# A softmax add on GpSimd, and two preparations moved behind later attention units

## The chip, the core and the metric

The kernel runs on one core of a Trainium2 chip. The core has TensorE (PE, matrix products into PSUM; its weight loads are shown as PEld), VectorE (DVE), ScalarE (ACT), GpSimd (POOL) and SyncE (SP, which here issues nearly all DMAs). Each engine works through its own instructions in order; between engines semaphores hold an instruction until its operands are there. The metric is the time on the device in microseconds. Before the change it was 2141.11 us, the median of three runs from 2140.84 to 2141.45.

## The reference

Attention with a sink and a window, then a mixture of experts in which every expert sees every token and a Sinkhorn iteration makes the weights:

```python
# q, k, v: (4, 8, 768, 64): batches, heads, positions, head size
scores = scale * q @ k.T
keep = (column < 4) | (0 <= row - column < 128)     # sink, or window
a = exp(where(keep, scores, -1e9) - max)
a = a / (sum(a) + 1e-9)
x = (a @ v) laid out as 3072 tokens x 512
P = exp(x @ w_gate - max)
8 times: P /= rowsum + 1e-9; P /= columnsum + 1e-9; P *= 3072 / 8
out = sum over 8 experts e of P[:, e] * (relu(x @ w1[e]) @ w2[e])   # w1: 512 x 1024, w2: 1024 x 512
```

## The kernel before

**Numbers.** Matrix products run on values in the fp32r format. Where full precision is wanted, a value is held as two halves, high and low: `split` (line 348) makes the high half with a copy on ScalarE and the low half as source minus high half on VectorE. A product is then three products (high-high, high-low, low-high).

**Attention units.** The attention works in 48 units: 4 batches, 6 blocks of 128 rows, and two halves of four heads (`units`, line 389). For a unit, `transpose_qk` transposes keys and queries of two pairs of heads in PE (L426) and splits them into the buffer KQ (high half L430 on ScalarE, low half L431 on VectorE). `scores` does two heads at a time (`pr` is 0 or 1): six products each pair (L461) of a row block with 260 columns (4 of the sink, 256 of two blocks), then per head a custom VectorE instruction that adds the mask, scales and finds the maximum (L464), then per head an exponential on ScalarE that also sums the row (L467), then 1e-9 is added to the two sums (L468), the reciprocal is taken (L469), and GpSimd multiplies the rows (L471). `transpose_p` transposes the scaled rows in PE (L482) and splits them (L350 is the line in `split`; the buffer is PT). `transpose_sinks` does the same for the sink columns (L496, L497 on GpSimd, L499 on PE, L501 on ScalarE). `values` multiplies with V (L520), which `split_v` splits on GpSimd (L440, L441), and copies the outcome to xr (L532), half on ScalarE and half on VectorE. `store_x` sends it to memory and, for the first third of the tokens, splits it into the blocks B (L540, L541).

**Order of the steps.** The loop from line 712 runs n from -2 to 50. A step n holds, in this order: loads for unit n+2; the scores of unit n+1; the first values of unit n-1; a piece of the fill; a piece of the gate; the transposes of keys and queries of unit n+2; the transposed probabilities of unit n; the second values of n-1; the sinks of n; a second piece of the fill. PE's instructions are issued in exactly this written order (`manual_schedule`). On the other engines a planner sets the order: it plays the program through with its own costs and gives an engine that is free the instruction earliest in the program of those that are ready. `tc.issue_after(ins)` holds what is traced inside it behind `ins` on the engine of `ins`, and on that engine only. It is an order of issue, with no wait for the end of `ins`.

**The fill.** From n = 5 on (`START`) every step gives PE two pieces of the first expert's products (`plain`): products with W1 (L599), a rectified value split into h (L604 on ScalarE, L605 on VectorE), products with W2 (L615). An expert has four units of 256 columns; the fill takes units 0 and 1 first, then 2 and 3. `load_plain` loads a unit's raw W1 and W2 and splits them in four pieces, two of W1 and two of W2 (the buffers are W and W2f). For units 0 and 1 the pieces are held: W1's behind the splits of attention units 1 and 2, W2's behind those of units 3 and 4, on both engines, since both instructions of a split are named:

```python
for ins in us[1 + 2 * (j // 2) + u]["split"]:
    held_back.enter_context(tc.issue_after(ins))
split(d, r)
```

In the program they stand in step 5, where the fill makes its first piece. For units 2 and 3 nothing holds them.

**The gate.** For the first third of the tokens the routing products (L561) use weights split by `split_gate` (line 308): four 128x128 fills with zero (L310), the high half (L311), the low half (L312) and a small matrix `sel` (L313), all on VectorE. It stands at the start of step 2, held behind unit 1's split on VectorE. For later tokens the raw weights are used.

**After the attention** (from about 300 us) come the rest of the first expert and the others, in products of 512 columns (L784, L1028, L1343) with an order of steps that is written out for every engine. None of it is touched.

Of the kernel before, what the change touches and what calls it, by code (L numbers as in the profile page):

```python
# [12 lines left out]
ALU = mybir.AluOpType  # L13
# [216 lines left out]
def tile_sink_attention_moe(ctx: ExitStack, tc: tile.TileContext, q, k, v, wg, w1, w2, out):  # L230

    nc = tc.nc
    B, H, S, D = q.shape
    N, DM = out.shape
    E, _, FF = w1.shape
# [18 lines left out]
    def f32(ap):  # L254
        return ap.bitcast(F32)
# [52 lines left out]
    def split_gate():  # L308
        for kc in range(KC):
            nc.vector.tensor_copy(wgr[:, kc, :], zero)  # L310
        nc.vector.tensor_copy(wgr[:, :, 0:E], wg_raw)  # L311
        nc.vector.tensor_sub(wgr[:, :, E:2 * E], wg_raw, f32(wgr[:, :, 0:E]))  # L312
        nc.vector.tensor_add(sel, ident[0:2 * E, 0:E], ident[0:2 * E, E:2 * E])  # L313
# [27 lines left out]
    def load_raw(rawp, e, u):  # L341
        r1 = rawp.tile([P, KC, UF], F32, name="r1")
        nc.sync.dma_start(r1, w1[e].rearrange("(k p) f -> p k f", p=P)[:, :, u * UF:(u + 1) * UF])
        r2 = rawp.tile([P, 2, DM], F32, name="r2")
        nc.sync.dma_start(r2, w2[e, u * UF:(u + 1) * UF, :].rearrange("(c p) d -> p c d", p=P))
        return r1, r2

    def split(dst, src):

        return nc.scalar.copy(dst[:, 0], src).ins, nc.vector.tensor_sub(dst[:, 1], src, f32(dst[:, 0])).ins  # L350
# [39 lines left out]
    us = {}  # L390
# [4 lines left out]
    def load_sinks(b):  # L395
        vs = seq[b] = att.tile([SK, D], F32, name="vs")
        for r0 in range(0, SK, NK):
            (nc.sync if b else nc.scalar).dma_start(vs[r0:r0 + NK, :], v[b, :, 0:SINK, :])
# [10 lines left out]
    def load_block(b, i):  # L409
        raws[b, i] = r = [att.tile([P, H, D], F32, name=nm) for nm in ("kr", "qr", "vr")]  # L410
        cuts = (0, HH, H) if (b, i) == (0, 0) else (0, H)
        for ts in (((r[0], k), (r[1], q)), ((r[2], v),)):
            for h0, h1 in zip(cuts, cuts[1:]):
                for t, src in ts:
                    nc.sync.dma_start(t[:, h0:h1, :], src[b, h0:h1, i * P:(i + 1) * P, :].rearrange("h p d -> p h d"))
# [28 lines left out]
    def scores(n, pr):  # L444

        b, i, hh = units[n]
        u = us[n]
        K, Q = KQ[hh][:, :, :, 0:CW], KQ[hh][:, :, :, CW:][:, :, :, turn_of(b, i)]
        if pr == 0:
            u["sc"] = att.tile([P, HH, CW], F32, name="sc", bufs=3)  # L450
            u["st"] = att.tile([P, 3, HH], F32, name="st", bufs=3)
        sc = u["sc"]
        nmx, sm, rs = (u["st"][:, j, :] for j in range(3))
        hs = range(2 * pr, 2 * pr + 2)
        p2 = slice(2 * pr, 2 * pr + 2)
        ps = {h: ps_st.tile([P, CW], F32, name="st") for h in hs}

        for j, (a, c) in enumerate(((0, 0), (0, 1), (1, 0))):
            for h in hs:
                r0 = (h % 2) * D  # L460
                nc.tensor.matmul(ps[h], lhsT=Q[r0:r0 + D, a, pr, :], rhs=K[r0:r0 + D, c, pr, :],  # L461
                                 start=(j == 0), stop=(j == 2))
        for h in hs:
            nc.vector.tensor_tensor_reduce(out=sc[:, h, :], in0=ps[h], in1=masks[place(b, i).start, min(i, 2)], op0=ALU.add, op1=ALU.min,  # L464
                                           scale=-scale, scalar=3.0e38, accum_out=nmx[:, h:h + 1])
        for h in hs:
            nc.scalar.activation(sc[:, h, :], sc[:, h, :], AF.Exp, bias=nmx[:, h:h + 1], scale=-1.0, accum_out=sm[:, h:h + 1])  # L467
        nc.vector.tensor_scalar(rs[:, p2], sm[:, p2], 1e-9, None, op0=ALU.add)  # L468
        nc.vector.reciprocal(rs[:, p2], rs[:, p2])  # L469
        for h in hs:  # L470
            u["scaled"] = nc.gpsimd.tensor_scalar(sc[:, h, :], sc[:, h, :], rs[:, h:h + 1], 1.0, op0=ALU.mult, op1=ALU.mult).ins  # L471
# [102 lines left out]
    def gate_step():  # L574
        if gates and next(gates[0], 0) == 0:
            gates.pop(0)
            gate_step()

    def load_plain(e, u):

        r1, r2 = load_raw(rawp, e, u)
        W1 = wa.tile([P, 2, KC, UF], F32R, name="W1")
        W2 = w2pr.tile([P, 2, 2, DM], F32R, name="W2f")
        for j, (d, r) in enumerate(((W1[:, :, 0:KH], r1[:, 0:KH]), (W1[:, :, KH:], r1[:, KH:]), (W2[:, :, 0], r2[:, 0]), (W2[:, :, 1], r2[:, 1]))):
            with ExitStack() as held_back:
                if u < 2:

                    for ins in us[1 + 2 * (j // 2) + u]["split"]:
                        held_back.enter_context(tc.issue_after(ins))
                split(d, r)  # L590
        return W1, W2
# [62 lines left out]
    def run_fill(k_):  # L654
        for _ in range(k_):
            next(fill, None)
# [5 lines left out]
    def load1(n):  # L662
        e, u = units0[n]
        R1[n] = rawp.tile([P, KC, UF], F32, name="r1")
        nc.sync.dma_start(R1[n], w1[e].rearrange("(k p) f -> p k f", p=P)[:, :, u * UF:(u + 1) * UF])
# [10 lines left out]
    def sums1(n):  # L676

        A11, A12, A21, A22 = blocks(R1[n])
        if n not in ST:
            ST[n] = new_sums()  # L680
        S = ST[n]
        nc.gpsimd.tensor_add(S[:, 3], A21, A22)
        nc.gpsimd.tensor_sub(S[:, 0], S[:, 3], A11)
        nc.gpsimd.tensor_sub(S[:, 2], A11, A21)
        nc.gpsimd.tensor_sub(S[:, 1], A12, S[:, 0])

    def pieces1(n):

        if n not in ST:
            ST[n] = new_sums()  # L690
        W = W1F[n] = (w1p if n % 2 else w1r).tile([P, 2, 7, KH, P], F32R, name="W1f")
        return [(W[:, :, 0:2].rearrange("p w a k f -> p w (a k) f"), R1[n][:, :, 0:P]), (W[:, :, 2], blocks(R1[n])[3]),
                (W[:, :, 3:5], ST[n][:, 0:2]), (W[:, :, 5:7], ST[n][:, 2:4])]
# [3 lines left out]
    def first_w1(n):  # L697

        if n == L - 8:
            load1(0)  # L700
        elif n == L - 6:
            sums1(0)
            first_pieces.extend(pieces1(0))
        if n >= L - 6 and first_pieces:
            split(*first_pieces.pop(0))
# [5 lines left out]
    with tc.manual_schedule(engines={PE}):  # L711
        for n in range(-2, L + 3):
            on = lambda j: 0 <= j < L
            if on(n + 2):
                b, i, hh = units[n + 2]
                if hh == 0:
                    with (tc.high_priority() if n == -2 else nullcontext()):
                        load_block(b, i)
                    if i == 0:
                        load_sinks(b)  # L720
            if n == -2:
                nc.sync.dma_start(wg_raw, wg.rearrange("(k p) e -> p k e", p=P))
            if n == 2:
                with tc.issue_after(us[1]["split"][1]):
                    split_gate()
            gates += later
            later.clear()
            if on(n + 1):
                scores(n + 1, 0)
                scores(n + 1, 1)  # L730
            if on(n - 1):
                values(n - 1, 0)
            if n >= START:
                run_fill(1)
            gate_step()
            for j in (0, 1) if n == -2 else (n + 2,) if n >= 0 else ():
                if on(j):
                    transpose_qk(j)
            if on(n):
                transpose_p(n, 0)  # L740
                with (tc.issue_after(us[n - 1]["scaled"]) if n > 1 else nullcontext()):
                    split_v(n)
            gate_step()
            if on(n):
                transpose_p(n, 1)
            if on(n - 1):
                values(n - 1, 1)
            gate_step()
            if on(n) and units[n][1]:
                transpose_sinks(n)  # L750
            if on(n) and units[n][1:] == (0, 1):
                with tc.issue_after(us[n]["scaled"]):
                    split_sinks(units[n][0])
            if n >= START:
                run_fill(1)
            first_w1(n)
        while gates:
            gate_step()
# [760 lines left out]
```

## Time and profile before

| | us |
|---|---|
| median of three runs | 2141.11 (2140.84 to 2141.45) |
| the profiled execution | 2141.32 |
| its span, first to last instruction | 2139.5 |
| TensorE busy | 2120.6 (99%) |
| VectorE busy | 1538.2 (72%) |
| ScalarE busy | 883.0 (41%) |
| GpSimd busy | 752.4 (35%) |

Times in the profile are microseconds from the start of the span. A row of the order of time has the start, the duration, the engine, the line, the operation, output<-inputs, shapes and how many were merged; in brackets is the idle time of the engine just before it and who ended it. A row of a group has the count, then busy time in us and the mean of one in ns, then the engine's idle time before them with its releasers. A row of waits has the total in us, how often, and the longest.

### The profile page before, as it was taken

What the parts mean: (1) busy time and instruction counts of PE and PEld (TensorE: products, weight loads), DVE (VectorE), ACT (ScalarE), POOL (GpSimd) and SP (SyncE); (2) the same over time, 40 slices, a digit from 0 to 9 for tenths busy, and PEclk for the clock granted to TensorE, in tenths of its full rate; (3) what the DMA queues carried; (4) which work ended last, traced back from release to release, by engine and by line L of the source; (5) the groups of instructions that cost most, each with busy time, mean ns of one, the idle gap of its engine ahead of it and who ended that gap; (6) DMA issues with size and microseconds to landing.
All of it is one profiled execution on the core that took longest, in us unless ns stands there. A gap on an engine that the chain in (4) does not pass through costs nothing.

```text
span 2139.5 us, 31828 instructions
## 1 busy us (share of the span) xinstructions
PE 2120.6 (99%) x10501; PEld 1770.4 (83%) x10501; DVE 1538.2 (72%) x2821; ACT 883.0 (41%) x1867; POOL 752.4 (35%) x950
## 2 busy tenths in 40 slices
PE   8999999999999999999999999999999999999998
PEld 7898897888888888888888888888888888888887
DVE  9878878877777776766666666666656666676666
ACT  7777744444444444442333223332333223332222
POOL 7766643233232331232223222232423232233223
PEclk9999999999999999999999999999999999999999
DMA  7434326999998987686666666667866666666662
GB/s 184 96 81 103 85 80 223 320 300 315 295 315 286 313 287 251 219 278 209 201 191 204 206 193 205 202 200 260 300 205 194 200 206 193 201 207 189 205 197 85
DMA packets 397643, 453.83 MB, mean 212 GB/s; under 512 B 99680, under 2 KB 265760, under 8 KB 396576
## 3 DMA queue, kind: packets, MB, share of 16 engines
q1 hardware_dynamic: 397080, 451.57, 67.8%
q8 instruction: 86, 1.41, 0.3%
q14 instruction: 85, 0.70, 0.1%
q10 hardware_dynamic: 392, 0.16, 0.0%
HBM read 314.17 MB, written 137.46 MB: 211 GB/s over the span
## 4 chain that ended last, share of the span: by engine, by line
PE 93%; DVE 3%; ACT 2%; POOL 1%; issue 0%; DMA 0%; SPq 0%; DVEq 0%; ACTq 0%; POOLq 0%
PE c L784 41%; PE o L1343 20%; PE held L1343 8%; PE o L1028 7%; PE held L1028 7%; PE O L520 3%; PE st L461 2%; ACT sc L467 1%; PE o L615 1%; PE st L482 1%; PE g L599 1%; PE st L426 1%; DVE sc L464 0%; POOL sc L471 0%; DVE PT L350 0%
## 5 line engine op out<-in xcount | busy, mean ns | idle before, releaser
L810 ACT CAST hf<-w 128x512 fp32r<-128x512 f32 x448 | 265.5, 622 | 561.8 <-POOL w L1310 298.9
L1343 PE MATMUL o<-hf,W2q 128*128 128x512 f32 x1920 | 472.0, 389 | 0.0
L1343 PEld LDWEIGHTS o<-hf,W2q 128*128 128x128 f32 x1920 | 360.0, 188 | 75.5 <-DVE acc L1357 0.9
L784 PE MATMUL c<-T,W1q 128*128 128x512 f32 x1530 | 388.9, 389 | 0.2 <-DVE w L1291 0.2
L811 DVE TENSOR_TENSOR hf<-w,hf 128x512 fp32r<-128x512 f32 x448 | 329.3, 763 | 76.2 <-ACT hf L810 68.5
L784 PEld LDWEIGHTS c<-T,W1q 128*128 128x128 f32 x1530 | 286.8, 188 | 60.7 <-DVE w L1291 0.9
L1357 DVE TENSOR_TENSOR acc<-o,acc 128x512 f32<-128x512 f32 x298 | 204.7, 688 | 171.1 <-PE o L1343 171.1
L784 PE MATMUL c<-B,W1q 128*128 128x512 f32 x1134 | 278.3, 389 | 0.0
L1310 POOL TENSOR_TENSOR w<-w 128x512 f32<-128x512 f32 x64 | 82.7, 1293 | 491.6 <-DVE w L1292 491.6
L784 PEld LDWEIGHTS c<-B,W1q 128*128 128x128 f32 x1134 | 212.5, 188 | 44.0
L1291 DVE TENSOR_TENSOR w<-c,M 128x512 f32<-128x512 f32 x192 | 132.3, 689 | 138.0 <-PE c L784 132.6
L1287 ACT COPY M<-c 128x512 f32<-128x512 f32 x192 | 112.7, 587 | 249.4 <-PE c L784 249.3
L1343 PE MATMUL held<-hf,W2q 128*128 128x512 f32 x768 | 194.8, 389 | 0.0
L784 PE MATMUL c<-T,W1f 128*128 128x512 f32 x672 | 171.2, 390 | 0.1
L1028 PE MATMUL held<-W2f,h 128*128 128x512 f32 x672 | 171.1, 390 | 0.0
L1028 PE MATMUL o<-W2f,h 128*128 128x512 f32 x672 | 170.6, 389 | 0.1
L1343 PEld LDWEIGHTS held<-hf,W2q 128*128 128x128 f32 x768 | 144.0, 188 | 29.8
L1325 POOL TENSOR_TENSOR w<-w 128x512 f32<-128x512 f32 x64 | 106.3, 1661 | 176.0 <-DVE hf L811 176.0
L1028 PEld LDWEIGHTS o<-W2f,h 128*128 128x128 f32 x672 | 126.0, 188 | 27.0 <-DVE acc L1035 0.9
L784 PEld LDWEIGHTS c<-T,W1f 128*128 128x128 f32 x672 | 125.7, 188 | 27.0 <-issue 0.5
L1028 PEld LDWEIGHTS held<-W2f,h 128*128 128x128 f32 x672 | 125.8, 188 | 26.4 <-DVE W2f L811 0.5
L837 POOL TENSOR_TENSOR r<-r 128x256 f32<-128x256 f32 x27 | 20.1, 746 | 359.2 <-ACT M L991 223.1
(216 smaller groups left out, 3104.5 us busy)
## 6 DMA issues: line engine op xcount, KB each, us to landing
W2q<-w2s SPq DMA_DIRECT2D x448, 256.0 KB, 3.2
W1q<-w1s SPq DMA_DIRECT2D x444, 256.0 KB, 2.9
w1s<-W1f SPq DMA_DIRECT2D x56, 896.0 KB, 7.8
w2s<-WT SPq DMA_DIRECT2D x136, 256.0 KB, 3.5
r<-in_moe_w_dram SPq DMA_DIRECT2D x64, 512.0 KB, 3.9
w2s<-W2f SPq DMA_DIRECT2D x56, 256.0 KB, 4.8
PB<-psd SPq DMA_DIRECT2D x16, 512.0 KB, 4.1
w2s<-W2f SPq DMA_DIRECT2D x56, 128.0 KB, 6.5
```

Of the source, the lines that this page charges most:

```text
L461: nc.tensor.matmul(ps[h], lhsT=Q[r0:r0 + D, a, pr, :], rhs=K[r0:r0 + D, c, pr, :], start=(j == 0), stop=(j == 2))
L520: nc.tensor.matmul(u["O"][:, pr], lhsT=x_, rhs=y_, start=(j == 0), stop=(j == len(ops) - 1))
L784: nc.tensor.matmul(ps, lhsT=w1(a, k), rhs=x[:, b, k, :], start=(start and j == 0), stop=(stop and j == len(TERMS) - 1), skip_group_check=n ...
L810: nc.scalar.copy(dst[:, 0], src)
L811: at(1, lambda: nc.vector.tensor_sub(dst[:, 1], src, f32(dst[:, 0])))
L1028: nc.tensor.matmul(o, lhsT=h[c, th][:, a, off:off + P], rhs=W2F[n][:, w, c, :], start=(begin and c == 0 and j == 0), stop=(end and c == 1 ...
L1287: nc.scalar.copy(t, T["c2"])
L1291: nc.vector.tensor_add(w, T["c1"], T[m])
L1310: nc.gpsimd.tensor_sub(S3, T["A11"], T["A21"])
L1325: at(k, lambda: nc.gpsimd.tensor_sub(T["A11"], w, T["A11"]))
L1343: nc.tensor.matmul(o, lhsT=W2Q[part, n, m][:, a, k * P:(k + 1) * P], rhs=F[part, n, H_OF[m]][:, w, :], start=(j == 0 and (begin or not hol ...
L1357: nc.vector.tensor_add(sums[m, k], o, sums[m, k])
```

## The change

Two things are changed, all within the attention stage. First, the add of 1e-9 to the two sums is issued on GpSimd; the instruction has a second operation, a multiplication by 1.0. The reciprocal stays on VectorE. Second, preparations move. The four W2 pieces of units 0 and 1 of the first expert are no longer traced with their W1 pieces but put in a list, `second_pieces`; at the end of step 5 the two of unit 0 are split, at the end of step 6 the two of unit 1, held behind `us[n]["split"][1]`, the VectorE instruction of attention unit n's last split. The W1 pieces stay behind units 1 and 2. `split_gate` moves from the start of step 2, behind unit 1, to the start of step 6, behind unit 5.

```diff
-        nc.vector.tensor_scalar(rs[:, p2], sm[:, p2], 1e-9, None, op0=ALU.add)
+        nc.gpsimd.tensor_scalar(rs[:, p2], sm[:, p2], 1e-9, 1.0, op0=ALU.add, op1=ALU.mult)
         nc.vector.reciprocal(rs[:, p2], rs[:, p2])
...
+    second_pieces = []
+
     def load_plain(e, u):
...
         for j, (d, r) in enumerate(((W1[:, :, 0:KH], r1[:, 0:KH]), (W1[:, :, KH:], r1[:, KH:]), (W2[:, :, 0], r2[:, 0]), (W2[:, :, 1], r2[:, 1]))):
+            if u < 2 and j >= 2:
+                second_pieces.append((d, r))
+                continue
             with ExitStack() as held_back:
                 if u < 2:
 
-                    for ins in us[1 + 2 * (j // 2) + u]["split"]:
+                    for ins in us[1 + u]["split"]:
                         held_back.enter_context(tc.issue_after(ins))
                 split(d, r)
...
-            if n == 2:
-                with tc.issue_after(us[1]["split"][1]):
+            if n == 6:
+                with tc.issue_after(us[5]["split"][1]):
                     split_gate()
...
             if n >= START:
                 run_fill(1)
+            if n in (5, 6):
+                with tc.issue_after(us[n]["split"][1]):
+                    for _ in range(2):
+                        split(*second_pieces.pop(0))
             first_w1(n)
```

## The prediction

> **What bounds the kernel now.** I read the page first, then busy time by stretch, then the groups of instructions of the first 300 us, then the instructions in order of time around the two places that the diff touches.
>
> ```profile
> PE 2120.6 (99%) x10501; PEld 1770.4 (83%) x10501; DVE 1538.2 (72%) x2821; ACT 883.0 (41%) x1867; POOL 752.4 (35%) x950
> ```
> ```profile
> 0.00:40.00 40.00, 31.70 (x190) 25.18 (x190) 35.23 (x127) 29.27 (x85) 30.43 (x83) 0.96 0.78 199
> 40.00:300.00 260.00, 257.47 (x2173) 231.91 (x2171) 209.66 (x746) 192.15 (x600) 168.18 (x386) 1.00 0.36 86
> 300.00:2139.50 1839.50, 1831.44 (x8144) 1513.29 (x8143) 1293.36 (x1949) 661.57 (x1182) 553.79 (x482) 1.00 0.73 230
> ```
> Over the whole span TensorE (PE) is busy 99%. The second fence has, per stretch, its length and then the busy time of PE, its weight loads, VectorE (DVE), ScalarE (ACT) and GpSimd (POOL). Everything that is edited lies in the attention stage, up to about 300 us. After it PE loses 8 us in 1839, so a shift of the stage's end passes to the end of the kernel one to one. In the first 40 us PE misses 8.3 us and DVE is the busiest; from 40 to 300 PE looks full, but busy time of pipelined matmuls hides waits, which stand at its weight loads:
>
> ```profile
> L461 PEld LDWEIGHTS st<-KQ 64*128 64x128 f32 x576 | 44.6, 192 | 25.9 <-DVE PT L350 9.0 <-DVE KQ L431 6.9 <-ACT PS L501 4.0
> L468 DVE TENSOR_SCALAR st<-st 128x2 f32<-128x2 f32 x96 | 21.0, 219 | 24.5 <-ACT sc L467 20.5
> ...
> L496 POOL TENSOR_SCALAR SS<-sc 128x16 fp32r<-128x16 f32 x80 | 15.1, 206 | 2.4
> L605 DVE SCALAR_TENSOR_TENSOR h<-g,h 128x256 fp32r<-128x256 f32 x24 | 9.8, 409 | 0.3
> ```
> ```profile
> PEld st L461 <- DVE PT L350: 9.0, 27, 0.4
> PEld st L482 <- POOL sc L471: 1.3, 4, 0.4
> ```
> So PE's scores (L461) wait, in 27 units, for the low half of the probabilities that DVE splits (L350). The scaling on POOL (L471) held PE back 4 times, for 1.3 us together. The stage is a ring from unit to unit: scores, four reduces on DVE (L464), four exponentials on ACT (L467), the high half of the next keys on ACT (L430), their low half on DVE (L431), two low halves of probabilities (L350), scores again. One turn shows it:
>
> ```profile
> 138.18 1.92 POOL L471 TENSOR_SCALAR sc<-sc,st 128x260 f32<-128x260 f32 x4 [2.02 <-ACT sc L467]
> 138.41 0.19 ACT L467 ACTIVATION_READ_ACCUMULATOR sc<-sc,st 128x1 f32 x1
> 138.63 0.59 ACT L430 CAST KQ<-st 128x512 fp32r<-128x512 f32 x1
> 138.63 0.17 DVE L468 TENSOR_SCALAR st<-st 128x2 f32<-128x2 f32 x1 [0.62 <-ACT sc L467]
> 138.83 0.17 DVE L469 RECIPROCAL st<-st 128x2 f32<-128x2 f32 x1
> 139.25 0.69 DVE L431 TENSOR_TENSOR KQ<-st,KQ 128x512 fp32r<-128x512 f32 x1 [0.26 <-ACT KQ L430]
> 139.86 1.28 DVE L350 TENSOR_TENSOR PT<-st,PT 128x512 fp32r<-128x512 f32 x2
> ```
> The second add waits 0.62 us at the head of DVE's queue for the exponential, yet nothing is lost: the low half behind it (L431) is waited for until ACT has made the high half, at 138.63 + 0.59 = 139.22. Between the reduces and L431 DVE stands in ACT's shade.
>
> **The add on GpSimd.** It takes 96 adds from DVE (21.0 us busy) and puts 96 on POOL, two per unit. POOL has no 128x2 row; the nearest is its tensor-scalar on 128x16, 0.206 us, which I take (DVE's own row is 0.219, so POOL pays 0.2 either way), 20 us on an engine that is busy 168 of 260. The 1.0 multiply behind the add is in the same instruction. Because the add's 0.62 us wait and 0.17 us run are in the shade, the steady gain is nothing. What is new is that the reciprocal (L469) waits for POOL. POOL runs in order: behind the first pair's two scalings (1.92 / 2 = 0.96 us from 138.18, so to 139.14) stands the second add, to about 139.35, if the planner keeps program order. The reciprocal can then start only some 0.1 us after L431 could, and the planner, which gives an idle engine the first ready instruction, puts it behind L431. There, in the ring's DVE part, it costs its issue slot:
>
> ```profile
> 43.43 0.15 DVE L469 RECIPROCAL st<-st 128x2 f32<-128x2 f32 x1
> 43.50 1.26 DVE L350 TENSOR_TENSOR PT<-st,PT 128x512 fp32r<-128x512 f32 x2
> ```
> that is 43.50 - 43.43 = 0.07 us. With the 27 units in which PE's scores wait for exactly this: 27 x 0.07 = **+1.9 us**. Bounds: 0 if it falls elsewhere, and the rival below if it stands ahead of L431. The scaling itself comes about 0.2 to 0.5 us later, behind a wait that held PE for 1.3 us in all, at the very start; I take 0 (up to 4 x 0.3 = 1.2).
>
> One place gains. In the third unit's turn the two adds took over 1.2 us each:
>
> ```profile
> 16.65 1.28 DVE L468 TENSOR_SCALAR st<-st 128x2 f32<-128x2 f32 x1
> 18.05 1.23 DVE L468 TENSOR_SCALAR st<-st 128x2 f32<-128x2 f32 x1
> 19.41 0.67 DVE L431 TENSOR_TENSOR KQ<-st,KQ 128x512 fp32r<-128x512 f32 x1
> 20.77 0.43 DVE L532 COPY xr<-O 64x256 f32<-64x256 f32 x1
> 21.22 1.49 DVE L310 CAST wgr<-zero 128x128 fp32r<-128x128 f32 x4
> ...
> 22.86 0.43 DVE L464 CUSTOM_DVE_ANT_0 sc<-st,mask 128x260 f32<-128x260 f32 x1
> ```
> ```profile
> 17.99 1.27 POOL L407 TENSOR_TENSOR VS<-vm,VS 32x512 fp32r<-32x512 f32 x1
> ...
> 19.08 0.51 PE L461 MATMUL st<-KQ 64*128 64x260 f32 x1
> 20.13 1.28 PE L461 MATMUL st<-KQ 64*128 64x260 f32 x11 [0.54 <-DVE KQ L431]
> ```
> The second add ends as POOL's instruction ends (18.05 + 1.23 = 19.28; 17.99 + 1.27 = 19.26). [...]
>
> PE's scores were started at 19.08 and went on at 20.13, so this is worth 20.13 - 19.08 = 1.05 us: **-1.05 us**. Everywhere else the stall is in the shade; the excess of all other adds, (0.219 - 0.170) x 96 - (1.28 + 1.23 - 2 x 0.17) = 2.5 us (0.170 is the add's undisturbed row above), is the bound of what more could come.
>
> **The routing weights.** Their seven DVE instructions stand behind unit 1 now: from the end of the copy at 21.20 to the first reduce at 22.86 the ring is late by 1.66 us. They go behind unit 5 with all of these instructions, and in the program they stand ahead of that unit's scores, as now. So the same reduce of a later unit waits the same time: -1.66 and +1.66, sum **0**. PE reads them from 64.4 us on, so behind unit 5, at about 45 us, isn't late:
>
> ```profile
> L561 PEld LDWEIGHTS O<-B,wgr x32: 187/188/192, 64.4 to 114.1; 128*128 128x128 f32 x32
> ```
> Bounds: -1.66 if the planner lets the reduces pass, +1.66 if unit 2 doesn't get shorter because something else is last there.
>
> **The W2 pieces.** Four pieces, each an ACT copy and a DVE subtract, held behind units 3 and 4. Now they run here:
>
> ```profile
> 35.35 1.04 DVE L350 TENSOR_TENSOR W2f<-r,W2f 128x512 fp32r<-128x512 f32 x1
> ...
> 36.42 0.56 ACT L430 CAST KQ<-st 128x512 fp32r<-128x512 f32 x1
> 37.12 0.68 DVE L431 TENSOR_TENSOR KQ<-st,KQ 128x512 fp32r<-128x512 f32 x1
> ```
> They fill the shade: ACT is done at 36.98, L431 starts at 37.12, so a pair costs about 0.1 us, two pairs **-0.2 us** when taken away. Before, their place in the program was unit 5's fill, after the reduces of the units whose shade they used. The new place is the end of steps 5 and 6, ahead of the next unit's scores, so a DVE that has just ended the probabilities takes them before the reduces. The trace has this case, W2 pieces of units 2 and 3 of the expert, that nothing holds back:
>
> ```profile
> 129.48 0.98 PE L461 MATMUL st<-KQ 64*128 64x260 f32 x12
> 141.38 0.39 PE L461 MATMUL st<-KQ 64*128 64x260 f32 x2
> ...
> 240.68 1.52 DVE L350 TENSOR_TENSOR W2f<-r,W2f 128x512 fp32r<-128x512 f32 x2
> 242.69 0.43 DVE L464 CUSTOM_DVE_ANT_0 sc<-st,mask 128x260 f32<-128x260 f32 x1
> 247.62 0.38 PE L461 MATMUL st<-KQ 64*128 64x260 f32 x1 [0.45 <-DVE KQ L431]
> 254.26 0.99 PE L461 MATMUL st<-KQ 64*128 64x260 f32 x12
> 255.01 1.65 DVE L350 TENSOR_TENSOR W2f<-r,W2f 128x512 fp32r<-128x512 f32 x2
> ...
> 260.63 0.39 PE L461 MATMUL st<-KQ 64*128 64x260 f32 x1
> ```
> A pair holds the reduces for 1.52 to 1.65 us. Not all of it stays: the two turns from 247.62 to 260.63 took 13.0 us, against 141.38 - 129.48 = 11.9 for two ordinary turns, so 1.1 us for the pair at 255.01 (in the turn ahead of 247.62 more was done, so I leave it out). I take 1.1 for each pair, **+2.2 us**, bounds 0 (shade) and 1.65 each. The pieces' ACT copies are no longer held at all, because the new hold names only the DVE instruction: ACT may make them earlier, in its idle stretches before the exponentials; I take 0, bound 4 x 0.56 = 2.2 if each of them delays an exponential (0.56 is ACT's 128x512 cast in the fence above). The raw W2 buffers come free later, and with them the loads of the next two on SP's queue; nothing reads those before W2 pieces are split again, in the second half of the stage.
>
> **The sum**: -1.05 - 0.2 + 0 + 2.2 + 1.9 = +2.85 us. The profiled execution took 2141.32 us (span 2139.5 and 1.8 around it), 0.2 over the median of the runs, 2141.11. So 2141.11 + 2.85 = about **2144 us**, +0.13%. I call 0.2% (4.3 us) what a measurement tells from no change; this is inside.
>
> **Rivals.** (1) *Slower: the reciprocal ahead of the keys.* If the planner believes POOL's add done before ACT's high half, L469 stands ahead of L431 in DVE's in-order queue, and on the chip L431 waits for POOL. Place: every unit from 7 on; it decides when the add ends later than 139.22 in the turn above. Exponentials end at 138.60 and the first scaling pair at 139.14; with the extra hop before the first add about 139.3, add to 139.5, reciprocal to 139.6: L431 loses 0.35 us. Likeliest are units where a DVE h (L605, 24 of them) stands between, which gives the reciprocal time to be ready first: 24 x 0.35 = 8.4 in place of the 1.9, 2150.5 us; in all 41 units 14.4, 2156.5 us. For it speaks that DVE waits 20.5 us for these sums already; against it that the planner's order in the trace follows the chip's closely. [...]
> (2) *Faster: what is moved lies in the shade.* The shade in the W2 fence holds 1.6 us; if the two pairs and the routing weights fall into it, and unit 2 is relieved, -1.05 - 1.66 - 0.2 = -2.9, 2138.2 us; with the other adds' 2.5 us of stalls on the ring after all, -5.4, 2135.7 us. Against it the rows at 21.22 and 240.68, where such pieces went first.
> (3) *Nothing to see.* PE is 99% busy; what the units lose or win is caught up where ACT or PE is last (13 to 14 units of 41), or the changes cancel: 2141 us.
>
> **Chances.** Forecast 0.42; (1) 0.26 (0.18 at 2150.5, 0.08 at 2156.5); (2) 0.20, of which 0.12 under the 0.2% line, because the same relief also reaches units 0 to 4 where DVE is full; (3) 0.12. The forecast's own range is 2141 to 2147 (its bounds: pairs 0 to 1.65 each, slot 0 to 1.9, ACT copies), and 0.04 of its upper end passes 0.2%. Faster 0.12, slower 0.26 + 0.04 = 0.30, the same 0.58. For 8 in 10 the range goes down to 2136.5 and up to 2151, which leaves out the all-units half of (1) and the last of (2).
>
> **What would show it.** In the changed profile: L468 on POOL at about 0.2 us; L469 idle for POOL, behind L431 in DVE's order (ahead of it: rival 1); the scores that follow those at 19.08, ahead of the fifth unit, come 2 to 3 us earlier; W2f and wgr on DVE in one block before the first reduce after unit 5, 3 us long, and a pair after unit 6. Wrong would be: these pieces between reduces and L431 (rival 2), or unit turns after 80 us longer by 0.3 us.

## The result, and the profile after

The changed kernel takes 2168.14 us (median of 4 runs, 2167.12 to 2169.73); the kernel before, on the same chip, 2141.2 us. The ratio is 1.0127, 95% interval 1.0109 to 1.0144: slower by about 27 us, against a forecast of 2144.0 us and a range that ended at 2151. The engines' row of the page after, and the same stretches as before, up to the attention stage's end, which now lies at about 328 us:

```profile
PE 2135.8 (99%) x10501; PEld 1781.7 (82%) x10501; DVE 1516.6 (70%) x2725; ACT 883.0 (41%) x1867; POOL 771.2 (36%) x1046
```
```profile
0.00:40.00 40.00, 29.42 (x171) 24.09 (x172) 25.40 (x98) 27.15 (x80) 31.30 (x88) 0.83 0.74 176
40.00:328.00 288.00, 274.74 (x2188) 244.04 (x2186) 197.34 (x678) 194.66 (x606) 187.06 (x477) 0.97 0.33 81
328.00:2167.10 1839.10, 1831.66 (x8146) 1513.59 (x8145) 1293.90 (x1950) 661.14 (x1182) 552.86 (x482) 1.00 0.73 230
```
The rest of the kernel is untouched: 1839.10 us after the stage, 1839.5 before. The whole loss lies in the stage, and it is not work: VectorE is busy 21.6 us less and GpSimd 18.8 us more, as forecast. In the first 40 us VectorE falls from 35.23 to 25.40 us: it waits, and so has done 98 instructions by then instead of 127 (some of the fewer are moved pieces, which run later). The waits of the first 370 us, in the kernel after (total, times, longest):

```profile
DVE st L469 <- POOL st L468: 84.7, 87, 2.6
PEld st L461 <- DVE KQ L431: 20.0, 20, 2.9
PE st L461 <- DVE KQ L431: 14.0, 14, 2.7
```
and the last two of them in the kernel before:

```profile
PEld st L461 <- DVE KQ L431: 6.9, 13, 0.9
PE st L461 <- DVE KQ L431: 2.2, 6, 0.5
```
VectorE stands 84.7 us at the head of its queue for GpSimd's add, in 87 of 96 reciprocals, and TensorE's scores wait for the keys' low half (L431), which stands behind the reciprocal: 14.0 us in place of 2.2, and at most 2.7 at a time in place of 0.5.

An ordinary turn of the kernel after, in order of time:

```profile
68.13 0.95 POOL L471 TENSOR_SCALAR sc<-sc,st 128x260 f32<-128x260 f32 x2 [0.30 <-DVE st L469]
68.36 0.19 ACT L467 ACTIVATION_READ_ACCUMULATOR sc<-sc,st 128x1 f32 x1
68.45 0.56 ACT L430 CAST KQ<-st 128x512 fp32r<-128x512 f32 x1
...
69.16 0.19 POOL L468 TENSOR_SCALAR st<-st 128x2 f32<-128x2 f32 x1
69.39 0.17 DVE L469 RECIPROCAL st<-st 128x2 f32<-128x2 f32 x1 [1.36 <-POOL st L468]
69.47 0.67 DVE L431 TENSOR_TENSOR KQ<-st,KQ 128x512 fp32r<-128x512 f32 x1
```
The high half of the keys is done at 68.45 + 0.56 = 69.01, but L431 starts at 69.47. In VectorE's order the reciprocal stands ahead of it and waits for the second add, which GpSimd starts at 69.16, since it does the first pair's two scalings first (68.13 + 0.95 = 69.08). The last exponential had ended at 68.55. So the queue's chain is add, reciprocal, two scalings, add, reciprocal, L431, and in this turn L431 is 0.46 us late. The order is the same in every turn from unit 7 on, and L431 starts 0.3 us or more after its high half in 38 of these 41 turns; in the kernel before in none.

A batch's start is worse. The turn at 98 us, kernel after:

```profile
97.06 1.04 POOL L403 TENSOR_TENSOR vm<-vs,bd 96x512 f32<-96x512 f32 x1
98.45 0.62 POOL L406 TENSOR_SCALAR VS<-vm 96x512 fp32r<-96x512 f32 x1
...
99.86 1.27 POOL L407 TENSOR_TENSOR VS<-vm,VS 32x512 fp32r<-32x512 f32 x1
...
100.67 0.56 ACT L430 CAST KQ<-st 128x512 fp32r<-128x512 f32 x1
101.20 0.73 POOL L541 TENSOR_TENSOR B<-xr,B 128x256 fp32r<-128x256 f32 x1
101.45 0.38 PE L461 MATMUL st<-KQ 64*128 64x260 f32 x1
102.02 0.19 POOL L468 TENSOR_SCALAR st<-st 128x2 f32<-128x2 f32 x1
102.25 0.17 DVE L469 RECIPROCAL st<-st 128x2 f32<-128x2 f32 x1 [2.62 <-POOL st L468]
103.54 0.19 POOL L468 TENSOR_SCALAR st<-st 128x2 f32<-128x2 f32 x1
103.76 0.17 DVE L469 RECIPROCAL st<-st 128x2 f32<-128x2 f32 x1 [1.35 <-POOL st L468]
103.84 0.67 DVE L431 TENSOR_TENSOR KQ<-st,KQ 128x512 fp32r<-128x512 f32 x1
104.57 1.25 PE L461 MATMUL st<-KQ 64*128 64x260 f32 x8 [2.73 <-DVE KQ L431]
```
The split of the sinks' values (L403, L406, L407; 2.93 us, once a batch) stands on GpSimd ahead of the first add, and L541 with it. The high half of the keys was ready at 101.23, L431 starts at 103.84, and TensorE stands 2.73 us. That stop costs more than its length; the stretches of the kernel after (length, TensorE, its loads, VectorE, ScalarE, GpSimd, granted clock):

```profile
103.00:104.00 1.00, 0.00 (x0) 0.00 (x0) 0.24 (x2) 0.00 (x0) 0.64 (x2) 0.91 1.24 281
105.00:110.00 5.00, 5.00 (x29) 4.77 (x28) 2.76 (x14) 3.47 (x11) 4.18 (x12) 0.50 0.23 52
```
and of the kernel before, where the same unit (15) runs:

```profile
91.00:96.00 5.00, 4.88 (x39) 4.26 (x39) 4.48 (x17) 3.83 (x15) 5.00 (x12) 1.00 0.72 161
```
The granted clock falls within the stop, at 103.81, 2.0 us after the stop's start at 101.84, and is 0.50 in the 5 us from 105 us, where TensorE does 29 matrix multiplications instead of 39. The rows that begin the scores of units 15 and 16 of the kernel before:

```profile
91.12 1.79 PE L461 MATMUL st<-KQ 64*128 64x260 f32 x12
96.90 0.39 PE L461 MATMUL st<-KQ 64*128 64x260 f32 x1 [0.25 <-DVE KQ L431]
```
In the kernel after unit 15 begins at 101.45 (quoted above) and unit 16 here:

```profile
112.00 1.00 PE L461 MATMUL st<-KQ 64*128 64x260 f32 x12
```
So unit 15 is 10.3 us late and unit 16 15.1: this one batch start costs 4.8 us. The table does the same subtraction for other units (start of the unit's first scores, less the same in the kernel before, us); units 16, 28 and 40 are the ones behind a batch's start, at which the scores of units 15, 27 and 39 are held. The last eight rows are experiments, told below.

| kernel | 3 | 6 | 7 | 10 | 15 | 16 | 27 | 28 | 39 | 40 | 42 | 47 |
|---|---|---|---|---|---|---|---|---|---|---|---|---|
| after | 1.9 | 3.6 | 3.6 | 8.6 | 10.3 | 15.1 | 16.7 | 21.6 | 22.8 | 26.2 | 26.5 | 27.8 |
| the add alone | 2.1 | 7.5 | 7.6 | 9.7 | 11.4 | 15.3 | 17.1 | 20.5 | 22.6 | 26.1 | 26.3 | 27.6 |
| the moves alone | -0.6 | -1.9 | -1.9 | 1.8 | 1.8 | 1.8 | 1.8 | 2.0 | 1.5 | 1.7 | 1.7 | 1.7 |
| add, sinks' split later | 1.8 | 5.6 | 5.6 | 7.7 | 9.4 | 13.3 | 18.2 | 21.4 | 25.9 | 29.1 | 29.9 | 31.1 |
| add, second reciprocal later | 1.6 | 3.7 | 4.1 | 4.5 | 4.8 | 8.9 | 8.3 | 10.4 | 10.0 | 13.6 | 14.1 | 14.4 |
| add, no sinks' split | 1.4 | 5.4 | 5.4 | 7.6 | 9.3 | 10.2 | 12.6 | 13.6 | 15.6 | 16.6 | 20.1 | 20.9 |
| add, second reciprocal later, no split | 1.3 | 1.3 | 1.7 | 2.2 | 2.5 | 2.6 | 2.9 | 3.0 | 2.5 | 2.6 | 5.0 | 5.3 |
| one add for four heads | 0.1 | 1.2 | 1.2 | 1.4 | 1.5 | 4.5 | 3.8 | 4.9 | 4.4 | 5.5 | 7.7 | 7.4 |
| no add | -1.2 | -2.4 | -2.4 | -2.6 | -2.6 | -2.7 | -2.7 | -2.7 | -2.5 | -2.5 | -2.7 | -3.0 |

After's row shows three kinds of loss: steps at units 16, 28 and 40 (4.8, 4.9 and 3.4 us), a creep of 0.1 to 0.35 us per unit between them, and 5 us between units 7 and 10, where the moved pieces now run; ahead of them 3.6 us are lost by unit 6, in the first batch's start.

The steps are a stop and a low clock together. Ahead of units 28 and 40 the stops are half as long as ahead of unit 16:

```profile
181.66 1.25 PE L461 MATMUL st<-KQ 64*128 64x260 f32 x8 [1.36 <-DVE KQ L431]
```
(and 1.35 us at 259.10), yet the granted clock is 0.50 for 6.83 us from 103.81, for 6.83 us from 182.32 and for 3.41 us from 260.83; between 40 and 300 us of the kernel before it is 1.00 throughout. The three stops (5.4 us) and half of the 17.1 us at 0.50 make 14.0 us, an estimate that takes TensorE as the bound in these stretches and half of its work as lost at 0.50; the three steps are 13.1 us.

### The profile page after: what moved, and what is told of

It reads as the page before. It is cut to its first block, busy times and chain, and to the rows that moved or that the text cites. A ratio compares the mean times of both kernels' runs of the same rounds, so it can differ in the third digit from the quotient of the medians.

```text
span 2167.1 us, 31802 instructions
## 1 busy us (share of the span) xinstructions
PE 2135.8 (99%) x10501; PEld 1781.7 (82%) x10501; DVE 1516.6 (70%) x2725; ACT 883.0 (41%) x1867; POOL 771.2 (36%) x1046
## 4 chain that ended last, share of the span: by engine, by line
PE 91%; DVE 4%; POOL 2%; ACT 2%; issue 1%; ACTq 0%; POOLq 0%; DVEq 0%
PE c L793 40%; PE o L1352 20%; PE held L1352 8%; PE held L1037 7%; PE o L1037 7%; PE O L520 2%; PE st L461 1%; PE st L482 1%; PE o L620 1%; POOL sc L471 1%; PE g L604 1%; ACT sc L467 1%; DVE PT L350 1%; PE st L426 1%; POOL st L468 0%
```

## The experiments

**Which part costs.** The first four kernels each do one part of the change.

The add alone, everything else as before:

```diff
-        nc.vector.tensor_scalar(rs[:, p2], sm[:, p2], 1e-9, None, op0=ALU.add)
+        nc.gpsimd.tensor_scalar(rs[:, p2], sm[:, p2], 1e-9, 1.0, op0=ALU.add, op1=ALU.mult)
```

> The add of 1e-9 on GpSimd alone; W2 pieces and routing weights stay where they were. Theory A (the add: the reciprocal stands ahead of the low half of the keys in VectorE's queue and waits for GpSimd, which runs in order): most of the 27 us comes with it. In the changed kernel the units gained about 4.4 us of lateness where the W2 pieces and the routing weights stand (units 7 to 9), so about 22 us are left: 2160 to 2166 us, with steps of 3 to 5 us where GpSimd splits the sinks of a new batch. Theory B (the moves: blocks of preparations ahead of the reduces): 2139 to 2143 us.

Measured 2168.97 us, ratio 1.0131 (1.0114 to 1.0148). The add alone has the whole loss, and its waits in the first 370 us are those of the whole change:

```profile
DVE st L469 <- POOL st L468: 85.2, 87, 2.6
PE st L461 <- DVE KQ L431: 13.3, 14, 2.8
```
That is 3 us above the range of the theory of the waiting reciprocal. The theory took off the 4.4 us that the whole change loses between units 7 and 9; by the table the add alone loses 7.5 us up to unit 6, where the whole change loses 3.6, so that the moves win early about what they cost later.

Both moves, the add as before (the change's other hunks, shown above):

```diff
             if u < 2 and j >= 2:
                 second_pieces.append((d, r))
                 continue
...
-            if n == 2:
-                with tc.issue_after(us[1]["split"][1]):
+            if n == 6:
+                with tc.issue_after(us[5]["split"][1]):
                     split_gate()
```

> The W2 pieces and the routing weights moved, the add stays on VectorE. Theory A: two W2 pairs ahead of the reduces cost 1.1 to 1.8 us each, the routing weights cost behind unit 5 at most what they cost behind unit 1 (1.7): +1 to +4 us, 2142 to 2145 us. Theory B: 2160 us or more.

Measured 2142.91 us, ratio 1.0012 (1.0002 to 1.0021): 1.7 us late at the stage's end. By the table the moves win 1.9 us up to unit 7 and then lose 3.7 us up to unit 10.

The W2 pieces alone (only the hunks of `second_pieces`, and the W1 pieces' hold):

```diff
-                    for ins in us[1 + 2 * (j // 2) + u]["split"]:
+                    for ins in us[1 + u]["split"]:
```

> Only the four W2 pieces moved behind units 5 and 6; routing weights and add as before. If the pieces hold the reduces there as the later ones did at 240.68 and 255.01: +2 to +3.5 us, 2143 to 2145 us. If they lie in ScalarE's shade: 2140.5 to 2141.5 us.

Measured 2143.91 us, ratio 1.0013 (1.0004 to 1.0023). Its VectorE in order of time, around the first pair:

```profile
45.10 0.42 DVE L610 SCALAR_TENSOR_TENSOR h<-g,h 128x256 fp32r<-128x256 f32 x1
45.45 1.83 DVE L350 TENSOR_TENSOR W2f<-r,W2f 128x512 fp32r<-128x512 f32 x2
47.20 0.41 DVE L464 CUSTOM_DVE_ANT_0 sc<-st,mask 128x260 f32<-128x260 f32 x1
```
The pair stands ahead of the reduces, as forecast, and keeps the first of them 47.20 - 45.52 = 1.7 us. The second pair, at 52.97, does the same. Unit 10's scores come 3.2 us late in this trace, so nearly all of 2 x 1.7 stays.

The routing weights alone:

```diff
-            if n == 2:
-                with tc.issue_after(us[1]["split"][1]):
+            if n == 6:
+                with tc.issue_after(us[5]["split"][1]):
                     split_gate()
```

> Only the split of the routing weights moved from behind unit 1 to behind unit 5. If it holds the reduces alike in both places: 2140.5 to 2142 us. If the new place is cheaper, as the changed kernel's 0.62 us for the four fills against 1.49 says: down to 2139.5 us. If unit 2 doesn't get shorter without it: up to 2143 us.

Measured 2140.99 us, ratio 1.0001 (0.9991 to 1.0011). In its trace unit 4 begins 1.9 us early and unit 10 0.2 late: what the old place gets back the new one pays.

**Why the add costs.** The next kernels all keep the add on GpSimd and leave the moves out. The first holds the sinks' split one unit longer:

```diff
-                with tc.issue_after(us[n]["scaled"]):
+                with tc.issue_after(us[n + 1]["scaled"]):
                     split_sinks(units[n][0])
```

> The add on GpSimd alone, and the split of the sinks' values (L403, L406, L407: 1.04, 0.62 and 1.27 us on GpSimd at a batch's start) held one unit longer, behind the scalings of the next unit, so that it no longer stands ahead of the add in GpSimd's queue. Theory Q (the vector engine's queue is the path, and the loss has two parts: about 0.15 to 0.2 us in every turn, and 3 to 5 us at each batch's start, where the add waits behind the sinks' split and the clock falls after TensorE's stop): the steps of 3.9, 3.4 and 3.5 us at units 16, 28 and 40 go, some 11 us, and perhaps 2 to 5 of the 7 us lost by unit 5; 2152 to 2158 us. Theory R (what costs is the longer round trip of add, reciprocal and scaling in every turn, 96 times, and the steps are only where it shows): 2165 to 2169 us.

Measured 2171.98 us, ratio 1.0143 (1.0128 to 1.0159): a miss, 14 us above the theory's range and 3 above the kernel it was to mend. The order of time shows why:

```profile
101.82 1.04 POOL L403 TENSOR_TENSOR vm<-vs,bd 96x512 f32<-96x512 f32 x1
...
105.00 0.19 ACT L467 ACTIVATION_READ_ACCUMULATOR sc<-sc,st 128x1 f32 x1
...
105.11 1.28 POOL L407 TENSOR_TENSOR VS<-vm,VS 32x512 fp32r<-32x512 f32 x1
106.47 0.72 POOL L541 TENSOR_TENSOR B<-xr,B 128x256 fp32r<-128x256 f32 x1
107.28 0.19 POOL L468 TENSOR_SCALAR st<-st 128x2 f32<-128x2 f32 x1
```
The split went behind the scalings it was held to and stands ahead of the next turn's adds instead. The first add now starts at 107.28, 2.1 us after the last exponential's end (105.19; it needs only the first two), and the loss spreads over two units: by the table it grows by 8.8 us from unit 15 to 27, against 5.7 with the split in its old place. The edit moves GpSimd's work from one turn to the next and takes it out of none. This leaves two readings, that the split is not the cause, or that it only collides elsewhere; they are told apart further on.

The second reciprocal and its scalings behind L431:

```diff
+        us[n]["low"] = nc.vector.tensor_sub(lo, src, f32(hi)).ins
...
+        if pr == 0:
+            scale_rows(n, 0)
...
+            if on(n + 1):
+                with (tc.issue_after(us[n + 2]["low"]) if n >= 0 and on(n + 2) else nullcontext()):
+                    scale_rows(n + 1, 1)
```

> The add on GpSimd alone, and the reciprocal and scalings of each unit's second pair of heads held behind the low half of the keys and queries (L431) of the same turn, so that L431 no longer waits for GpSimd; the sinks' split stays where it is. The scalings come some 0.7 us later by it; the transposes that read them start 4 us after. Theory Q: the 0.15 to 0.2 us of every turn go (about 9 us over units 7 to 47), and the stops at the batches' starts shrink by one of their two round trips, since L431 then stands behind the first pair's reciprocal alone (103.52 instead of 104.96 us at unit 16): 1.4 us of TensorE's stop at each of three, 2 with the clock; 2150 to 2158 us. Theory R: the round trip is longer still, so 2169 to 2175 us.

Measured 2155.32 us, ratio 1.0067 (1.0052 to 1.0082): 13.7 us better than the add alone, inside the queue theory's range and far from its rival's, by which a longer round trip costs more. The creep is gone (table: 4.5 us at unit 10, 4.8 at unit 15). The steps stay, at 4.1, 2.1 and 3.6 us: that each would shrink by 2 us (from 3.9, 3.4 and 3.5) came true in part at unit 28 alone. The time fell into the range by the creep, as expected, and by 3.5 us won ahead of unit 7, which was not.

Both together:

> Both of the last two at once, the add still on GpSimd. Theory Q: nothing that L431 stands behind waits for GpSimd any more, but for the first pair's reciprocal, whose add is done long before; the whole loss goes: 2140 to 2146 us. Theory R: 2165 us or more.

The edit is the last two diffs. Measured 2160.37 us, ratio 1.0088 (1.0073 to 1.0104): a miss, 5 us worse than the reciprocal's move alone: L431 still stands behind the first pair's reciprocal, and that one waits for the add behind the moved split. In its trace, in unit 16's turn, this reciprocal waits 4.05 us (to 104.41) and TensorE stands 2.73 us for L431.

**Is it the sinks' split?** Three kernels ask it: one takes the split away from the kernel before (a control), one from the add alone, one from the add with the later reciprocal.

```diff
+    VS0 = att1.tile([SK, H * D], F32R, name="VS")
...
     def split_sinks(b):
-        vm = att1.tile([SK, H, D], F32, name="vm")
-        nc.gpsimd.tensor_tensor(vm, ...)
-        VS = seq[b] = att.tile([SK, H * D], F32R, name="VS")
...
-        nc.gpsimd.tensor_scalar(VS, vmf, 1.0, 1.0, op0=ALU.mult, op1=ALU.mult)
-        nc.gpsimd.tensor_sub(VS[2 * NK:], ...)
+        seq[b] = VS0
```

> The kernel before, the add on the vector engine, without the split of the sinks' values: the three instructions L403, L406 and L407 (2.94 us of GpSimd for each of the four batches) are left out, and one tile of zeros stands in for what they make; their loads and every matrix multiplication stay. A control: before, only the scalings stand behind the split, and the transposes that read them come about 4 us later. All theories: 2139.5 to 2141.5 us.

Measured 2139.39 us, ratio 0.9993 (0.9984 to 1.0003). That is 0.1 us below the range. With the add on VectorE the split costs 1.3 us by the medians, and the interval includes no difference at all.

> The add on GpSimd alone, and the split of the sinks' values left out in the same way. Theory Q2 (holding the split one unit longer only moved the collision one turn on, since 2.94 us of it fit in no turn of a GpSimd that is busy for 4 of 5 us; the steps at the batches' starts are the split's, as the add stands behind it): the steps of 3.9, 3.4 and 3.5 us at units 16, 28 and 40 go, and a part of the 7 us by unit 5; 2152 to 2158 us. Rival S (the steps come at a batch's start from something else, its first block's loads or its 4 transposes in place of 8): 2165 to 2169 us.

Measured 2160.31 us, ratio 1.0089 (1.0071 to 1.0107): 8.7 us better than with the split, 2.3 above the range I gave. The steps at 16, 28 and 40 are 0.9, 1.0 and 1.0 us by its trace, against 3.9, 3.4 and 3.5 with the split. Up to 1.3 of the 8.7 us may be the split's own cost, by the control. The same batch start as above, without the split:

```profile
100.55 0.17 DVE L467 RECIPROCAL st<-st 128x2 f32<-128x2 f32 x1 [1.36 <-POOL st L466]
...
100.63 0.67 DVE L429 TENSOR_TENSOR KQ<-st,KQ 128x512 fp32r<-128x512 f32 x1
...
101.36 1.29 PE L459 MATMUL st<-KQ 64*128 64x260 f32 x11 [0.60 <-DVE KQ L429]
```
(L429 is L431 here, two lines up.) TensorE stands 0.60 us instead of 2.73 (2.77 in the add alone), and the granted clock is 1.00 on the mean from 100 to 150 us. The rival, that something else of a batch's start makes the steps, falls.

> As add_rcp_later (the add on GpSimd, the second pair's reciprocal behind L431; 2155.3 us), and the split of the sinks' values left out. Theory Q2: both parts of the loss are gone, 2155.3 less 3.3, 2.1 and 3.6 us of steps, and up to 3 us of unit 2's: 2142 to 2147 us. Rival S: 2153 to 2156 us.

Measured 2145.75 us, ratio 1.0024 (1.0015 to 1.0034). With both mechanisms away 23.2 of the add's 28.2 us are back; taken one at a time they gave 13.7 and 8.7, so they add up nearly. Of the 5 us that are left, 1.3 are there by unit 3 and 2.5 come between units 39 and 42. There GpSimd forms sums of the next weights, in front of the add (this kernel, L466 is L468):

```profile
247.85 1.21 POOL L690 TENSOR_TENSOR r<-r,r 128x256 f32<-128x256 f32 x1
249.14 0.19 POOL L466 TENSOR_SCALAR st<-st 128x2 f32<-128x2 f32 x1
```
The reciprocal waits 0.90 us for this add, TensorE then stands 1.26 us for the keys' low half (to 250.98), and the granted clock, 1.00 from 50 to 250 us, is 0.97 on the mean from 250 to 300. That the sums are the cause is still argued, not shown: no run took them away.

**Fewer round trips.** One add and one reciprocal for all four heads, behind the last exponential, the sinks' split in its place:

```diff
+        if pr == 0:
+            return
-        nc.gpsimd.tensor_scalar(rs[:, p2], sm[:, p2], 1e-9, 1.0, op0=ALU.add, op1=ALU.mult)
-        nc.vector.reciprocal(rs[:, p2], rs[:, p2])
-        for h in hs:
+        nc.gpsimd.tensor_scalar(rs, sm, 1e-9, 1.0, op0=ALU.add, op1=ALU.mult)
+        nc.vector.reciprocal(rs, rs)
+        for h in range(HH):
```

> The add on GpSimd, but one add and one reciprocal for all four heads of a unit, behind the last exponential, in place of one for each pair; the sinks' split stays. The chain from the last exponential to L431 is then add and reciprocal alone (0.09 + 0.19 + 0.03 + 0.17 us), not also the first pair's two scalings (0.95 us), so L431 waits for the cast L430 (0.6 us after the last exponential) as it did before. Theory Q2: the part of every turn goes, the steps at the batches' starts stay with one round trip in place of two: 2150 to 2157 us, as when the second reciprocal was put behind L431. Theory R (every hop between the engines costs, wherever it stands): half as many hops, so half of the loss, about 2155 us too, but spread evenly over the units and with steps of 3 to 4 us at units 16, 28 and 40 unchanged.

Measured 2148.03 us, ratio 1.0033 (1.0021 to 1.0045): 20.9 us better than the add for each pair, 2 better than I expected. A turn of it:

```profile
61.24 0.56 ACT L430 CAST KQ<-st 128x512 fp32r<-128x512 f32 x1
61.42 0.19 POOL L470 TENSOR_SCALAR st<-st 128x4 f32<-128x4 f32 x1 [1.18 <-ACT sc L467]
61.65 0.18 DVE L471 RECIPROCAL st<-st 128x4 f32<-128x4 f32 x1 [1.46 <-POOL st L470]
...
61.84 0.69 DVE L431 TENSOR_TENSOR KQ<-st,KQ 128x512 fp32r<-128x512 f32 x1
```
VectorE waits as long as before for GpSimd (1.46 us), but L431 starts at 61.84, 0.04 us after ScalarE's high half is done (61.80). By the table it creeps 0.3 us from unit 6 to unit 15, against 3.9 of the add alone. The theory that each hop between the engines costs, wherever it stands, is out: half the hops left almost no creep, not half of it. The steps at 16, 28 and 40 shrank too (3.0, 1.1 and 1.1 us); that this is because only one add is left to wait for behind the split is argued.

**What the move could have won at most.** No add on any engine:

```diff
-        nc.vector.tensor_scalar(rs[:, p2], sm[:, p2], 1e-9, None, op0=ALU.add)
-        nc.vector.reciprocal(rs[:, p2], rs[:, p2])
+        nc.vector.reciprocal(rs[:, p2], sm[:, p2])
```

> The kernel before without the add of 1e-9 on any engine: the reciprocal is taken of the sums themselves (the largest exponential of a row is 1, so the sum is at least 1, and 1e-9 is below its rounding in fp32). It prices the add on the vector engine, and so what moving it could win at most. Theory Q: the add is 0.07 us in most turns and stood in the shade of the exponentials; only the two that stretched to 1.23 and 1.28 us in unit 2 count: 2139.5 to 2141 us, the same or up to 1.5 us faster than before. Rival (the vector engine is the bound of the whole first stage): 48 turns by 2 x 0.07 us and the stretched adds, 2132 to 2136 us.

Measured 2139.03 us (11 runs, 2137.89 to 2140.44) against 2140.99, ratio 0.9992 (0.9983 to 1.0002). That is half a us below the range, and far from the rival's. By the medians the 96 adds on VectorE cost 2 us, nearly all of it in the first seven units (table), and by the interval 3.6 at most. It has the lowest median of the study, but that it beats the kernel before isn't shown.

## Why the prediction was wrong

- **The step that failed** is "the planner ... puts it behind L431". I reasoned that an idle VectorE takes L431 first because the second add would be done 0.1 us later than the high half. The planner's order, which is fixed before the run, has the reciprocal ahead of L431 in every turn from unit 7 on, as in the turn at 69.39 and in the collision at 103.76, so L431 pays GpSimd's full queue. The +1.9 us of that step stand against 28.2 us measured for the add alone. This is rival 1, to which I gave 0.26. Its mechanism was right, and its price only for the creep: 0.35 us a turn, against about 0.5 us that L431 is late in the median turn, of which about 0.2 us a unit stays. Putting the second reciprocal behind L431 won 13.7 us, near the 14.4 of its wider case, but that is luck: of the 13.2 us that the table has at unit 47, 8.7 are creep (the narrower case had 8.4), 3.5 were won ahead of unit 7 and 1.0 in the steps. What stood against it, that the planner's order follows the chip's closely, was no evidence: the order seen before was made with the add on VectorE.
- **What no case had** is GpSimd's other work. I priced the wait by the turn's own scalings, with GpSimd free ahead of the first add. The row of L407 in unit 2 was quoted in the prediction, beside the add on VectorE that ended with it (19.28 and 19.26); that the moved add would stand behind that same instruction in GpSimd's queue follows from the same row and was not drawn. It is worth 8.7 us, most of it in three steps in which TensorE stops for 2.73, 1.36 and 1.35 us and the granted clock is 0.50 afterwards; no term of the sum and no rival had the clock.
- **"-1.05 us" in unit 2** did not come. The add itself is 0.19 us now, but in the kernel after the unit's first add waits behind L407 and L431 starts later than it did:

```profile
19.19 1.27 POOL L407 TENSOR_TENSOR VS<-vm,VS 32x512 fp32r<-32x512 f32 x1
20.55 0.19 POOL L468 TENSOR_SCALAR st<-st 128x2 f32<-128x2 f32 x1
...
22.37 0.67 DVE L431 TENSOR_TENSOR KQ<-st,KQ 128x512 fp32r<-128x512 f32 x1
```
  At 22.37 instead of 19.41; unit 3 begins 1.9 us late. The kernel without any add begins it 1.2 us early, so the term's size was right for an add that is gone, and wrong for one that waits elsewhere.
- **"+2.2 us" for the W2 pairs, and -0.2 for their old place**: the place (ahead of the reduces) was right, the term mis-sized. It measured about 3 us in time (2143.91 against 2140.76) and 3.2 at unit 10: each pair took 1.83 us there, not 1.52 to 1.65, and all of its 1.7 us stayed on the path, the upper bound I gave rather than the 1.1 I took. The -0.2 is not seen: with the W2 pieces alone unit 7 begins 0.1 us late.
- **"0" for the routing weights** was right, with its two halves: 1.9 us won by unit 4, and lost again by unit 10. In the kernel after, the fills themselves are shorter, 0.62 us where they took 1.49:

```profile
51.10 0.62 DVE L310 CAST wgr<-zero 128x128 fp32r<-128x128 f32 x4
```
- **ACT copies at 0, a shift of the stage's end one to one**: the second holds, as the stretch after the stage is 1839.1 us against 1839.5. No run has the copies by themselves, but the pairs' 2 x 1.7 us leave nothing for them.

## What to carry to other kernels

A small operation moved to an idle-looking engine is priced by two queues: everything that stands ahead of it on the new engine, in the worst turn and not the mean one, and everything that stands behind its consumer on the old one. Ask first where the consumer stands in its queue against the instruction on the critical path; here the move cost 28 us, where doing without the operation altogether won 2 by the medians, which the noise doesn't tell from nothing. If the hop has to stay, make it rarer and put it behind the critical instruction: one add for four heads took back 21 of 28 us, and the second reciprocal behind the critical instruction 14.

## What the runs showed of the hardware

- During a stop of TensorE of 2.73 us (from 101.84) the granted clock fell to 0.50 at 103.81 and stayed there for 6.83 us, and the next unit's lateness grew by 4.8 us: the other 2 us of the batch start's price came after the stop. Stops of 1.36 and 1.35 us at the next two batch starts were followed by a fall too. In the 3.41 us (the length of the shortest of the three stays at 0.50) ahead of each of the three falls TensorE was busy for 1.44, 2.05 and 2.06 us. So here stops of 1.36 and 1.35 us went with a fall, and in the same kernel one of 1.38 us, from 34.20, with none: the clock is 1.00 from 28.8 to 100 us. What decides it was not tested.
- The clock column says 1.00 for the first 10 us of both kernels, and the rows don't bear it out: a product of the scores (L461) takes 0.42 us there, as it does later at 0.50 (kernel after, 16 us), and 0.28 us at 1.00 from 27 us on in the kernel before. The first 40 us of the two kernels can't be compared by that column.
- The add's row on GpSimd is 0.19 us for 128x2 and for 128x4 alike, and the reciprocal starts 0.23 us after the add's start (69.16 and 69.39, 61.42 and 61.65). The hop by itself was short; what cost was the place in the two queues. On VectorE the add's row was 0.17 us in the prediction's turn; by the medians of 96 rows it is 0.170 us there and 0.191 on GpSimd.
- The four fills on VectorE took 1.49 us from 21.22 in the kernel before, where GpSimd worked without a break, and 0.62 from 51.10 in the kernel after, where it had nothing to do from 50.63 to past the fills' end. The rows of GpSimd before:

```profile
21.19 0.41 POOL L440 TENSOR_SCALAR V<-vr 128x256 fp32r<-128x256 f32 x1
...
21.90 0.73 POOL L441 TENSOR_TENSOR V<-vr,V 128x256 fp32r<-128x256 f32 x1
```
  and the last one ahead of the fills after:

```profile
49.49 1.14 POOL L541 TENSOR_TENSOR B<-xr,B 128x256 fp32r<-128x256 f32 x1
```
  That GpSimd's rows made the fills longer is not shown: no run took them away from beside the fills.
